# Five more pairs of idle products between the first turns and scores of a tuned attention and FFN kernel

## The chip, the cores and the metric

One core of one Trainium2 chip. The metric is device time in microseconds (us) of one execution, and a profile is one profiled execution with its own trace; times inside it count from the start of its span. TensorE is PE in the profile, VectorE DVE, ScalarE ACT, GpSimd POOL, SyncE SP. "Granted clock" is the share of TensorE's full clock that the trace records as granted.

## The reference

Chunked linear attention with decay, then a highway FFN on its output (cut):

```python
# attention: q, k, v of (4, 8, 768, 64), decay lam per head, blocks of 64
intra = einsum(qb, kb) * Dmask ;  intra = einsum(intra, vb)
inter = einsum(qb * lam_pow, kv_state)
out[block] = intra + inter
kv_state = lam_block * kv_state + einsum(kb * rev_pow, vb)
# FFN on x of (3072, 512)
H = maximum(x @ w_h, 0);  T = sigmoid(x @ w_t + b_t)
return T * H + (1 - T) * x
```

## The kernel before

The kernel builds a list of tasks and issues them in a fixed global order, `ORDER`; each engine gets its own tasks in that order. There are 12 steps, each 256 rows of one batch. A step loads k, q, v, casts or scales them (`kb`, `qb`, `vs`), turns k and q on TensorE, copies the turned tiles out of PSUM, where this kernel's products land (`kT`, `qT`), makes scores, masks them on DVE (`m`), and does intra, state (`kv`) and inter products. FFN products (`block`) and the final turns follow. Steps 0 and 1 are loaded in halves.

The parts that the change and the argument touch:

```python
NF = 12
...
def fill(eng):                                   # an idle pair: its result is never read
    for i in range(2):
        T.matmul(get("fill")[:, i], lhsT=id128, rhs=id128[:, None, :].to_broadcast([128, NP, 128]), start=True, stop=True)

buf(("fill",), "o", [128, 2, NP, C], F32, pool=ps)
for i in range(NF):
    task("fill", fill, writes=[("fill",)])
...
def trans(x, n, p, hs): ...                      # turns: 4 or 8 products of 128x128
def scores(n, u): ...                            # 16 products of 64x64 with 128 columns
def inter(n): ...                                # o <- ss, qT
def block(x, w, g, js): ...                      # FFN: w is wh or wt, the cast weights
...
issued = set()
for i in ORDER:
    t = tasks[i]
    assert all(d in issued for d in t.deps)
    issued.add(t)
    t.emit(t.eng)
```

In the kernel before, all twelve idle pairs come ahead of the first turn, to have TensorE at full clock by then: in its trace the clock is full from 4.21 us, and the first turn starts at 7.97.

## Time and profile before

| | before |
|---|---|
| time, median | 113.19 us (113.16 to 113.62) |
| span of the profiled run, mean granted clock | 110.9 us, 0.950 |
| first turn of step 0, first turn of step 2 | 7.97, 20.64 us |
| clock at half | 14.45 to 24.69 us |
| first FFN product | 24.80 us |

From the first FFN product on TensorE has no gaps to speak of (busy 15.20 of 15.20 us from 24.80 to 40, 20.00 of 20 to 60, 30.00 of 30 to 90), so the moment at which it starts, and the speed of the products before and after it, set the time. The prediction below shows the lines and how they are read.

### The profile page before, as it was taken

The page shows a single profiled execution, that of the slowest core. Times are in us where ns is not written, and L with a number is a line of the kernel's source. Part 1 is how long each engine was busy: PE and PEld are TensorE (multiplying, and loading weights), DVE is VectorE, ACT ScalarE, POOL GpSimd, SP SyncE. Part 2 cuts the span into 40 slices and gives each one's busy share as a digit, 9 for nine tenths or more (in the row PEclk, how much of TensorE's full clock was granted, in tenths as well). Part 3 has the DMA queues.
Part 4 walks back from the last instruction along what each step waited for, and adds up shares of the span by engine and source line. Part 5 has one row for each costly group of instructions (what it writes and reads, how often), then busy time and mean ns, then how long its engine had stood idle before and what let it go on. Part 6 is the DMA issues. An engine that isn't in the chain of part 4 may idle for free.

```text
span 110.9 us, 4776 instructions
## 1 busy us (share of the span) xinstructions
PE 101.5 (92%) x2073; PEld 86.3 (78%) x2073; DVE 78.4 (71%) x128; ACT 72.9 (66%) x137; POOL 63.5 (57%) x55
## 2 busy tenths in 40 slices
PE   4996489689999999999999999999999999999960
PEld 1353469578889889888888889999899888889950
DVE  0179896684998899797778854788775797764630
ACT  3574443177288967668695788787878844785780
POOL 6004626263469899988979979899940040401420
PEclk9999965559999999999999999999999999999998
DMA  0999999999999999999999999999995250024263
GB/s 10 267 292 290 290 293 287 293 356 320 253 290 297 288 292 292 290 294 289 293 287 287 279 292 295 292 264 370 392 343 204 107 188 0 6 101 183 101 236 142
DMA packets 43964, 27.57 MB, mean 249 GB/s; under 512 B 1828, under 2 KB 41000, under 8 KB 43944
## 3 DMA queue, kind: packets, MB, share of 16 engines
q1 hardware_dynamic: 43792, 27.27, 88.3%
q8 instruction: 16, 0.26, 1.0%
q14 instruction: 4, 0.03, 0.1%
q10 hardware_dynamic: 152, 0.01, 0.1%
HBM read 20.98 MB, written 6.29 MB: 246 GB/s over the span
## 4 chain that ended last, share of the span: by engine, by line
PE 76%; SPq 11%; DMA 6%; DVE 2%; issue 1%; POOLq 1%; ACT 0%; DVEq 0%
PE w L293 39%; SPq L208 11%; PE w L315 10%; PE w L223 10%; DMA kf<-in_k_dram 6%; PE w L239 5%; PE o L264 5%; PE kv L272 4%; PE o L252 4%; DVE qT L175 1%; POOLq L469 1%; DVE kb L175 1%; DVE hmx L297 0%; ACT o_sb L173 0%; DVEq L175 0%
## 5 line engine op out<-in xcount | busy, mean ns | idle before, releaser
L293 PE MATMUL w<-xT,w_b 128*128 128x256 bf16 (+1 forms) x416 | 46.9, 265 | 0.0
L293 PEld LDWEIGHTS <-w_b 128*128 128x128 bf16 x416 | 36.5, 98 | 4.4
L243 DVE TENSOR_TENSOR m<-w,tri 128x512 bf16<-128x512 f32 x48 | 30.8, 684 | 4.2 <-PE w L239 3.8
L309 POOL TENSOR_TENSOR th<-t_sb,hmx 128x512 bf16<-128x512 bf16 (+1 forms) x13 | 15.1, 1165 | 23.5 <-DVE hmx L297 14.4
L217 POOL TENSOR_TENSOR vs<-vf,pow_k 128x1024 bf16<-128x1024 f32 (+1 forms) x11 | 20.1, 1824 | 12.2 <-DMA vf<-in_v_dram 11.1
L297 DVE SCALAR_TENSOR_TENSOR hmx<-w,xT 128x512 bf16<-128x512 f32 (+1 forms) x26 | 16.5, 646 | 7.7 <-PE w L293 7.4
L217 POOL TENSOR_TENSOR qb<-qf,pow_q 128x1024 bf16<-128x1024 f32 (+1 forms) x11 | 19.2, 1746 | 4.2 <-DMA qf<-in_q_dram 4.2
L306 ACT ACTIVATE w<-w,bt_col 128x256 f32<-128x256 f32 (+1 forms) x26 | 11.2, 432 | 7.6 <-PE w L293 5.7
L173 ACT ACTIVATE xT<-o 128x512 bf16<-128x512 f32 x22 | 12.1, 597 | 3.7 <-PE o L264 2.3
L173 ACT ACTIVATE kT<-w 128x1024 bf16<-128x1024 bf16 (+1 forms) x11 | 10.0, 906 | 6.9 <-PE w L223 6.9
L315 PE MATMUL w<-id,th 128*128 128x128 bf16 x96 | 12.9, 219 | 0.6 <-POOL th L309 0.6
L239 PE MATMUL w<-qT,kT 64*64 64x128 bf16 x384 | 12.8, 231 | 0.7 <-ACT kT L173 0.3
L315 PE MATMUL w<-id,xT 128*128 128x128 bf16 x96 | 12.9, 220 | 0.0
L173 ACT ACTIVATE o_sb<-w 128x512 f32<-128x512 f32 (+1 forms) x17 | 9.6, 575 | 4.8 <-PE w L315 4.6
L306 ACT ACTIVATE t_sb<-w,bt_col 128x256 bf16<-128x256 f32 (+1 forms) x26 | 10.5, 458 | 3.0 <-PE w L293 3.0
L309 DVE TENSOR_TENSOR th<-w,hmx 128x512 bf16<-128x512 f32 (+1 forms) x13 | 8.4, 648 | 4.2 <-ACT w L306 4.0
L223 PE MATMUL w<-id,kb 128*128 128x128 bf16 x96 | 8.5, 231 | 2.8 <-DVE kb L175 1.4
L272 PE MATMUL kv<-vs,kb 64*64 64x64 bf16 x320 | 10.4, 203 | 0.1
L315 PEld LDWEIGHTS <-th 128*128 128x128 bf16 x96 | 9.4, 98 | 0.9 <-POOL th L309 0.8
L239 PEld LDWEIGHTS <-kT 64*64 64x64 bf16 x384 | 9.1, 112 | 1.2 <-ACT kT L173 0.5
L272 PEld LDWEIGHTS <-kb 64*64 64x64 bf16 x320 | 8.8, 117 | 1.3 <-issue 1.0
L315 PEld LDWEIGHTS <-xT 128*128 128x128 bf16 x96 | 9.3, 98 | 0.5
(46 smaller groups left out, 118.9 us busy)
## 6 DMA issues: line engine op xcount, KB each, us to landing
vf<-in_v_dram SPq DMA_DIRECT2D x24, 256.0 KB, 5.4
kf<-in_k_dram SPq DMA_DIRECT2D x24, 256.0 KB, 5.5
qf<-in_q_dram SPq DMA_DIRECT2D x24, 256.0 KB, 5.5
out_dram<-o_sb SPq DMA_DIRECT2D x23, 256.0 KB, 3.5
w_f<-in_moe_w_t_dram SPq DMA_DIRECT2D x4, 256.0 KB, 6.1
w_f<-in_moe_w_h_dram SPq DMA_DIRECT2D x4, 256.0 KB, 6.2
out_dram<-o_sb SPq DMA_DIRECT2D x2, 128.0 KB, 1.9
lam_bc<-in_lam_dram ACTq DMA_DIRECT2D x1, 4.0 KB, 3.5
```

The lines of the kernel that those rows point to most:

```text
L173: A.activation(dst, src, AF.Copy)
L208: nc.sync.dma_start(out=get(x, n, p)[:, h - hs.start:h - hs.start + 4, :], in_=src[b, h:h + 4, c * 2 * C:(c + 1) * 2 * C, :].rearrange("h ...
L217: ENG[eng].tensor_tensor(dst[:, hs], in0=get(x, n, p).rearrange("p h (j d) -> p h j d", j=J), in1=pw[:, :, :, None].to_broadcast([128, hs. ...
L223: T.transpose(get(x + "tr", n, p)[:, i, j, :], get(x + "b", n)[:, j, h:h + 2, :], id128)
L239: T.matmul(get("s", n, u, e)[half(b), i, j, :], lhsT=turned("k", n)[half(e), hp, b * C + j:(b + 1) * C:J], rhs=turned("q", n)[half(e), hp, ...
L243: V.tensor_tensor(get("m", n, u)[:, e], in0=get("s", n, u, e), in1=tri[:, None].to_broadcast([128, 2, J, C]), op=ALU.mult)
L272: T.matmul(get("kv", n // NST)[half(e), hp, :], lhsT=get("kb", n)[half(b), j, 2 * hp + e, :], rhs=get("vs", n)[half(b), 2 * hp + e, j, :], ...
L293: T.matmul(get(x, g, js[0])[:, i, :], lhsT=w[:, kc, j * 128:(j + 1) * 128], rhs=get("xT", g)[:, kc, :], start=(kc == 0), stop=(kc == KC - 1))
L297: V.scalar_tensor_tensor(get("hmx", g, js[0]), in0=get("h", g, js[0]), scalar=0.0, in1=get("xT", g)[:, js[0]:js[-1] + 1, :], op0=ALU.max, ...
L306: A.activation(get(*gate(g, js))[:, i, :], get("t", g, js[0])[:, i, :], AF.Sigmoid, bias=bt_col[:, j:j + 1])
L309: ENG[TH[js[0] // len(js) % 2]].tensor_tensor(get("th", g)[:, js[0]:js[-1] + 1, :], in0=get(*gate(g, js)), in1=get("hmx", g, js[0]), op=AL ...
L315: T.matmul(get("x", n, b, p)[:, (j - js[0]) * 128:(j - js[0] + 1) * 128], lhsT=get(x, g)[:, j, r * C:(r + 1) * C], rhs=id128, start=(j == ...
```

## The change

The intent is to keep TensorE's clock up. Between the first turns and the first FFN products TensorE has gaps, and the clock falls to half in that stretch. Five more idle pairs are put into the gaps of step 0. The schedule was made anew for it.

```diff
-NF = 12
+NF = 17
 ORDER = [ ... ]      # 537 -> 542 numbers; in TensorE's order this is:
  turn k, part 0
+ fill
  turn q, part 0
+ fill
  turn q, part 1
+ fill
  turn k, part 1
+ fill
  scores, first half
+ fill
  scores, second half
```

Everything else of TensorE's order and of the loads' order is the same. On the other engines some neighbours swap, and two stores change places. Early swaps: DVE scales both halves of step 1's v before it copies xT of step 0 (before: after it). ACT copies a second state (`ss`) of step 0 before its half of xT, and one mask of step 1 comes later on DVE.

## The prediction

> **What bounds the kernel now.** I read four views. First the page, for the strip of 40 slices and the chain that ended last.
>
> ```profile
> PE   4996489689999999999999999999999999999960
> PEclk9999965559999999999999999999999999999998
> DMA  0999999999999999999999999999995250024263
> ...
> PE 76%; SPq 11%; DMA 6%; DVE 2%; issue 1%; POOLq 1%; ACT 0%; DVEq 0%
> ```
>
> One slice is 110.9 / 40 = 2.77 us. From about 25 us to about 105 us TensorE never stops (nines) at full clock, so in that stretch its own work sets the time. Before 25 us it has gaps, and in slices 5 to 8 the granted clock is half. The DMA engines are full from 3 us on. That early stretch is the only place where the change can act.
>
> Second, the chain in order of time, to see what sets the moment at which TensorE becomes continuous:
>
> ```profile
> 12.35 0.83 SPq L208
> 13.18 0.04 issue
> 13.23 6.57 DMA kf<-in_k_dram
> ...
> 19.89 0.70 DVE kb L175
> 20.59 0.05 issue
> 20.64 1.90 PE w L223 x16
> 22.54 0.02 issue
> 22.56 1.24 DVE qT L175
> 23.80 0.04 issue
> 23.84 0.63 PE w L239 x13
> ```
>
> Up to 19.8 us the chain is loads issued one behind the other (0.83 us each), ending with the k block of step 2. Only then come the turns of step 2 (20.64), their copy, the scores (23.84), and at 24.87 the FFN products. What TensorE does before 20.64 is beside the chain as long as it is finished by 20.64.
>
> Third, stretches cut where the clock changes. I looked at 0.1 us steps and found the falls and rises at about 4.2, 14.46 and 24.70 us; the last two are 10.24 us apart, three times 3.41, so I cut in 3.41 us steps through those points. Columns: start:end, length, busy us (and count) of PE, PEld, DVE, ACT, POOL, then granted clock, DMA share, GB/s.
>
> ```profile
> 7.63:11.05 3.42, 2.46 (x51) 1.51 (x49) 3.02 (x7) 1.33 (x3) 1.21 (x2) 1.00 1.22 291
> 11.05:14.46 3.41, 1.64 (x61) 1.36 (x57) 3.12 (x7) 1.45 (x3) 2.43 (x3) 1.00 1.22 290
> 14.46:17.88 3.42, 3.19 (x67) 2.69 (x69) 3.19 (x7) 0.99 (x4) 0.83 (x1) 0.50 1.21 295
> 17.88:21.29 3.41, 2.51 (x55) 2.27 (x55) 1.89 (x4) 0.91 (x2) 1.07 (x1) 0.50 1.04 286
> 21.29:24.70 3.41, 3.09 (x76) 2.75 (x74) 2.50 (x4) 2.34 (x4) 2.10 (x2) 0.50 1.03 341
> ```
>
> A window with PE busy 2.46 of 3.42 us (72%) kept the clock; one with 1.64 (48%) lost it; at half clock 3.19 and 2.51 did not bring it back, and 3.09 did. So busy time alone is not the measure (3.19 failed, 3.09 succeeded): the failing window is mostly 64x64 products, the succeeding one has more 128x128 turns and dense 64x128 ones.
>
> Fourth, PE in order of time around the change:
>
> ```profile
> 7.97 0.39 PE L223 MATMUL w<-id,kb 128*128 128x128 bf16 x4
> 8.20 0.87 PE L223 MATMUL w<-id,qb 128*128 128x128 bf16 x8
> 9.60 0.40 PE L223 MATMUL w<-id,kb 128*128 128x128 bf16 x4 [0.54 <-DVE kb L175]
> 9.93 0.42 PE L239 MATMUL w<-qT,kT 64*64 64x128 bf16 x16
> 10.69 0.42 PE L239 MATMUL w<-qT,kT 64*64 64x128 bf16 x16 [0.34 <-ACT kT L173]
> 12.50 0.40 PE L223 MATMUL w<-id,kb 128*128 128x128 bf16 x4 [1.39 <-POOL kb L175]
> ```
>
> The gaps (0.54, 0.34, 1.39 us) are what the new products are meant to fill.
>
> [...]
>
> **The change, part by part.** It removes nothing. The built programs show TensorE's order unchanged except five added pairs of 128x512 products on the identity: after the turn of k part 0, after q part 0, after q part 1, after k part 1, and between the two halves of the scores, all of step 0. The loads keep their order. Some neighbours swap on the other engines; the one that matters is early on DVE: before, qT, bt_col, xT, then the two vs scalings of step 1; after, qT, vs, vs, xT, bt_col.
>
> Cost of a pair: the last 18 of today's 24 products start between 4.0 and 7.8 us, 3.8 / 17 = 0.22 us each, so 0.44 us a pair, 2.2 us for five. Step by step, with 0.23 us for four turns (7.97 to 8.20) and about 0.3 for 16 scores: k0 7.97 to 8.20, pair to 8.64, q0 to 8.87, pair to 9.31, q1 to 9.54, pair to 9.98, k1 to 10.21 (today starts 9.60), pair to 10.65, first scores start 10.65 (today 9.93), to 10.95, pair to 11.4, second scores 11.4 (today 10.69). So 1.5 us of the 2.2 go into gaps and 0.7 us is pushed down.
>
> The masks start 0.45 us after the scores (10.38 against 9.93): now 11.1; four take 2.48, to 13.6 (was 12.86). qT of step 1 to 14.2. Then the two vs scalings come first; today these run 14.50 to 15.84 on late v data, so they end at 15.5 to 15.8; then xT (0.6) to about 16.4. The first inter products wait for that xT (today's wait: 0.55 us on DVE xT, start 14.63). So they start at about 16.4 instead of 14.63. The run from them to the last scores of step 1 took 5.1 us (14.63 to 19.74), all at half clock.
>
> The window 11.05 to 14.46 gains 0.35 us of added products and the second scores; idle are about 0.7 (11.8 to 12.5) and 0.3 us (13.3 to 13.6), so about 2.4 of 3.41 busy, 70%, near the 72% that kept the clock. I choose "kept" at 60%. The next, to 17.88, then has TensorE idle for nearly 2 us until 16.4 and loses the clock at 17.88. Until then 1.4 us at full clock do 2.8 of those 5.1 us; the rest takes 2.3 us to about 20.2, before 20.64. No loss, no gain yet. The window 17.88 to 21.29 is then denser than today's (less was done before), and may restore the clock at 21.29 instead of 24.70.
>
> What that would be worth: ten of the sixteen turns, the scores (0.63) and the kv products (0.39) at double speed, so the FFN products start at about 23.8 instead of 24.87, 1.1 us earlier. But the third group of the next 32 (27.51 to 31.11, 8 in 0.87 us) starts at 27.51 + 2 x 0.87 = 29.25 and needs the first half of w_t, whose last cast on POOL ran 28.26 to 28.88 behind loads on full DMA engines. So TensorE would stop there for the weights: of 1.1 us at most 29.25 - 28.88 = 0.37 us is left. From there to the end it is work without gaps. The sum: between 0 and -0.4 us.
>
> **The rivals.** (a) The window to 14.46 still falls below the limit (48% lost it, 70% is untested): then the late xT costs, since 16.4 + 5.1 = 21.5 against 20.64: +0.7 to +0.9 us, perhaps recovered by an earlier rise. (b) The clock returns a window later than today (28.1): 3.4 us of FFN products at half speed, 1.7 us more, together +2 us. Against it: that window would be dense work, as the one that succeeded today. (c) The clock never falls: PE's work becomes faster, but the k block still lands at 19.8 and the weights at 28.3, so again -0.4 us. For it: that is the intent; against: nearly 2 us idle before 16.4. (d) The phase of the window differs from run to run: today's timed runs lie within 113.16 to 113.62 and the profiled one took 112.8, so phase is worth under 1 us. (e) The swaps later on cost or give some tenths, since TensorE has no slack there.
>
> **Range and chances.** Weights: about 45% for -0.2 to -0.4, 25% for about 0, 25% for +0.3 to +0.9, 5% for +2. Centre a little below today: 113.1 us, range 112.5 to 114.0. Over 2% faster would need -2.3 us, which the weights' landing forbids: 0.02. Over 2% slower needs rival (b): 0.04. Within 2%: 0.94.
>
> **What would show each step.** Right: scores of step 0 near 10.65 and 11.4; inter products near 16.4 after a wait on DVE xT; clock full across 14.46; k of step 2 still landing near 19.8; FFN products earlier than 24.87 and a new TensorE wait on POOL w_b near 28.9. Wrong: weights that land well before 28, or FFN products that start earlier and whose lead survives to the end (gain above 0.4), or a clock still half after 24.7.

Three things in the text were assumptions when it was written. The step of 3.41 us was one gap of 10.24 us divided by three; the later profiles bear it out, with half-clock stretches of 6.83, 10.24 and 13.65 us (e5, before, e7), two, three and four such steps. That the phase differs from run to run, in rival (d), showed afterwards: the first rise came at 4.21, 5.07 and 5.62 us in three profiles of before. That a window 70% busy would keep the clock, and that there is a "limit", was my estimate from one window that kept it at 72% and one that lost it at 48%; the later windows are not sorted by that share ("Still open" below).

## The result, and the profile after

| | before | changed |
|---|---|---|
| time, median | 113.19 us (113.16 to 113.62) | 111.84 us (111.70 to 112.25) |
| span of the profiled run, mean clock | 110.9 us, 0.950 | 110.2 us, 1.000 |
| first FFN product | 24.80 us | 23.91 us |

The ratio is 0.9878, interval 0.9841 to 0.9914. A ratio is the mean time of one kernel's fast runs over that of the other's of the same rounds, so not quite the ratio of the medians. The change made the kernel faster by 1.2%; I had predicted 113.1 us with a range from 112.5. The measured median lies below the range.

The page of the changed kernel, with the same rows as shown of before: forty slices (PE busy, granted clock, DMA busy), and the chain that ended last by engine.

```profile
PE   4999877579999999999999999999999999999960
PEclk9999999999999999999999999999999999999999
DMA  0999999999999999999999999999997340024264
...
PE 71%; SPq 12%; DMA 6%; POOL 5%; issue 1%; DVE 1%; POOLq 1%; ACT 0%
```

The clock row is where the two pages differ: the 6555 of slices 5 to 8 (counted from 0) is gone. In this profile the clock never falls while there is work.

TensorE in order of time (start, us, engine, line, operation; in brackets the idle time before and who ended it):

```profile
8.30 0.39 PE L223 MATMUL w<-id,kb 128*128 128x128 bf16 x4
8.52 0.59 PE L198 MATMUL o<-id 128*128 128x512 bf16 x2
8.95 0.39 PE L223 MATMUL w<-id,qb 128*128 128x128 bf16 x4
...
11.01 0.42 PE L239 MATMUL w<-qT,kT 64*64 64x128 bf16 x16
11.36 0.60 PE L198 MATMUL o<-id 128*128 128x512 bf16 x2
11.89 0.42 PE L239 MATMUL w<-qT,kT 64*64 64x128 bf16 x16
12.48 0.40 PE L223 MATMUL w<-id,kb 128*128 128x128 bf16 x4 [0.17 <-POOL kb L175]
...
15.33 0.24 PE L252 MATMUL o<-qT,ss 64*64 64x128 bf16 x2 [0.48 <-ACT ss L173]
...
20.62 0.62 PE L223 MATMUL w<-id,kb 128*128 128x128 bf16 x8 [1.48 <-DVE kb L175]
...
23.91 1.92 PE L293 MATMUL w<-xT,w_b 128*128 128x256 bf16 x16
```

The pairs sit where they were meant to, and the wait before the first turn of step 1 has shrunk from 1.39 to 0.17 us. The first inter products (15.33) wait for ACT's ss, not for DVE's xT. The turns of step 2 start at 20.62, as in before (20.64), because the k block lands when it landed before. What follows runs at full speed, so the FFN products come 0.89 us earlier. What ends last ahead of them is no longer the k block. The chain now comes from step 2's v block, which POOL scales before the kv products:

```profile
14.91 6.54 DMA vf<-in_v_dram
21.49 0.09 issue
21.59 1.92 POOL vs L217
23.50 0.04 issue
23.54 0.44 PE kv L272 x16
```

The v block landed at 14.91 + 6.54 = 21.45 us and its scaling ended at 23.51. In this profile a faster TensorE ahead of it could have brought little more: its scores before the kv products ended at 23.00 + 0.42 = 23.42.

The three windows in which the fall could have come, cut at this run's own steps (columns as in the prediction):

```profile
11.69:15.10 3.41, 2.46 (x75) 1.79 (x73) 3.41 (x6) 1.32 (x3) 1.78 (x3) 1.00 1.22 291
15.10:18.52 3.42, 2.58 (x88) 2.12 (x90) 3.42 (x8) 2.14 (x5) 1.49 (x1) 1.00 1.20 292
18.52:21.93 3.41, 1.94 (x54) 1.58 (x56) 2.21 (x5) 0.59 (x1) 0.76 (x2) 1.00 1.02 278
```

They are 72, 76 and 57% busy. The steps do not lie where they lay in before: in that run the clock first rose at 4.21 us, in this one at 4.86, and every later change sits whole steps of 3.41 us after the first rise (in before 14.45 and 24.69 us are three and six steps after it).

POOL's casts of the half of w_t that is loaded last and needed second. It holds the first half of the columns: the prediction calls it "the first half of w_t", the experiments below, by the order of loading, "the second half":

```profile
26.64 0.61 POOL L175 CAST w_b<-w_f 128x512 bf16<-128x512 f32 x1 [0.88 <-DMA w_f<-in_moe_w_t_dram]
27.41 0.62 POOL L175 CAST w_b<-w_f 128x512 bf16<-128x512 f32 x1 [0.16 <-DMA w_f<-in_moe_w_t_dram]
```

They end at 28.03 us, against 28.88 in before. The prediction had let them cap the gain; here the weights came 0.85 us earlier, and the lead of 0.89 us passed them whole.

Later some of the lead is lost. The chain in order of time, at the one place where it leaves TensorE in the middle of the run:

```profile
63.14 1.90 POOL qb L217
65.04 1.46 POOL kb L175
...
66.54 1.07 PE w L223 x16
```

In before these turns start at 67.26, so the lead is 0.72 us here, and 0.65 us at the last wait for DVE's hmx (106.07 against 105.42). That agrees with the spans' difference of 0.7 us. The medians differ by 1.35 us: one profile of each kernel does not hold the whole difference of the timed runs, and the experiments show why.

### The profile page after: what moved, and what is told of

The parts are those of the page before. It is cut to its first block, busy times and chain, and to the rows that moved or that the text cites. A ratio compares the mean times of both kernels' runs of the same rounds, so it can differ in the third digit from the quotient of the medians.

```text
span 110.2 us, 4797 instructions
## 1 busy us (share of the span) xinstructions
PE 100.9 (91%) x2083; PEld 84.4 (77%) x2083; DVE 78.5 (71%) x128; ACT 73.2 (66%) x137; POOL 63.9 (58%) x55
## 4 chain that ended last, share of the span: by engine, by line
PE 71%; SPq 12%; DMA 6%; POOL 5%; issue 1%; DVE 1%; POOLq 1%; ACT 0%
PE w L293 37%; SPq L208 12%; PE w L315 9%; PE w L223 8%; DMA vf<-in_v_dram 6%; PE o L264 5%; PE w L239 4%; PE kv L272 4%; PE o L252 3%; POOL vs L217 2%; POOL qb L217 2%; POOL kb L175 1%; DVE hmx L297 1%; POOLq L469 1%; ACT o_sb L173 0%
## 5 line engine op out<-in xcount | busy, mean ns | idle before, releaser
L239 PE MATMUL w<-qT,kT 64*64 64x128 bf16 x384 | 11.7, 220 | 0.6 <-DVE qT L175 0.6
L198 PE MATMUL o<-id 128*128 128x512 bf16 x34 | 10.0, 439 | 1.4 <-POOL id masks.py:199 1.4
L272 PE MATMUL kv<-vs,kb 64*64 64x64 bf16 x320 | 9.4, 194 | 0.4 <-DVE ss L175 0.3
L239 PEld LDWEIGHTS <-kT 64*64 64x64 bf16 x384 | 8.3, 106 | 1.6 <-issue 1.3
L223 PE MATMUL w<-id,kb 128*128 128x128 bf16 x96 | 7.7, 220 | 1.9 <-DVE kb L175 1.5
```

Source lines behind the costliest of these rows:

```text
L223: T.transpose(get(x + "tr", n, p)[:, i, j, :], get(x + "b", n)[:, j, h:h + 2, :], id128)
L239: T.matmul(get("s", n, u, e)[half(b), i, j, :], lhsT=turned("k", n)[half(e), hp, b * C + j:(b + 1) * C:J], rhs=turned("q", n)[half(e), hp, ...
L272: T.matmul(get("kv", n // NST)[half(e), hp, :], lhsT=get("kb", n)[half(b), j, 2 * hp + e, :], rhs=get("vs", n)[half(b), 2 * hp + e, j, :], ...
```

## The experiments

My theory after the result: the pairs keep the clock, the swaps do nothing for it, and how much that gives depends on how early the weights land. The rivals: the swap that frees the inter products gives the gain (swaps); it was luck in the phase (phase: how long after the start of the span the first rise comes, 4.16 to 7.22 us in these profiles; a window is a stretch of 3.41 us counted from it); what counts is something other than busy time (work). Order edits are given as TensorE's or the loads' order, since the numbers of `ORDER` tell nothing. Every run was correct. In the lists of clocks, mean clock 1.00 is no half-clock time; 0.969 is about 6.8 us of it, as (1 - 0.969) x 110.5 / 0.5, two windows; 0.954 is about 10.2 us, three windows, part of which can lie after the last product. The mean leaves out the time before the first rise, which the records do not cover.

**e1_fills_only** (the kernel before, with the pairs alone)

```diff
-NF = 12
+NF = 17
+ the five pairs at the changed kernel's places; other engines keep before's order
```

> The kernel before, in its own order, with nothing but the five added pairs at the same five places of TensorE's order (TensorE's order is then that of the changed kernel, the other engines keep theirs). Clock theory: [...]the granted clock stays at or near 1.00 through 25 us, the first FFN product starts near 24.0 us and the time is 0.985 to 0.991 of before, as the changed kernel's 0.988. Swap rival (the gain comes from the first inter products being freed of their wait for DVE's xT): 0.997 to 1.003, because that wait is in this kernel again.

Ratio 0.9946 (0.9879 to 1.0013). Mean clocks 0.954, 0.966, 0.969, 0.969, 1.00, 1.00; the eleven runs of before in these rounds 0.939 to 0.955. The clock half of the expectation holds in part: five of six runs lie above every run of before (the sixth was a slow run), but only two kept the clock throughout. The gain in time is unclear and smaller than expected. The profiled run shows one reason: its first rise was at 4.40 us, the clock fell at 18.05 and came back at 24.88. TensorE around that:

```profile
20.68 1.04 PE L223 MATMUL w<-id,kb 128*128 128x128 bf16 x8 [0.74 <-DVE kb L175]
...
24.88 1.92 PE L293 MATMUL w<-xT,w_b 128*128 128x256 bf16 x16
```

The turns of step 2 are at half clock and the FFN products start where they start in before (24.80). I infer that a half clock that ends before 20.6 us would cost little, and that one that covers 20.6 to 24.9 costs the gain in the FFN products' start; no run isolates either.

**e2_swaps_only** (the changed kernel without the five pairs)

```diff
-NF = 17
+NF = 12
- the five pairs; other engines keep the changed kernel's order
```

> The changed kernel without the five added pairs: only the swaps among neighbours on the other engines are left. Clock theory: the clock falls near 14.5 us as before and stays half for two or three windows (mean clock about 0.95), time 0.997 to 1.004 of before. Swap rival: 0.985 to 0.992.

Ratio 1.0075 (1.0012 to 1.0138). Mean clocks 0.939 to 0.954 in all six runs, as before. Alone the swaps neither keep the clock nor give the gain; they are a little slower, more than I expected. With e1 this settles that the pairs are what changes the clock. Whether the swaps add to the time once the pairs are there is not separated: the interval of e1 overlaps that of the changed kernel.

**e3_fills_in_hole** (the kernel before, three pairs in one gap)

```diff
  scores of step 0, second half
+ fill, fill, fill
  turn k of step 1
```

> The kernel before with three pairs (six products, about 1.3 us) in one place only: after the second scores of step 0, in the 1.39 us gap before the first turn of step 1. No score and no mask is delayed by them. Clock theory by share of busy time: the window that fell with 1.64 of 3.41 us busy has about 2.9 then, the clock stays up there, but the later gaps (14.1 to 14.6, 17 to 20.6) are as in before; the changed kernel held the clock with a window 57% busy, so it should hold here too: mean clock 0.97 to 1.00 and 0.985 to 0.993 of before. A rival, that the clock needs dense work from the first turns on (7.6 to 11 us) and not a filled gap later: falls as before, 0.997 to 1.003.

Ratio 0.9965 (0.9883 to 1.0048) from three fast runs; three others were slow. Clocks 1.00, 0.992, 0.985, 0.97, 0.956, 0.941. Filling one later gap can keep the clock too, in some runs: the three fast ones have 0.985 to 1.00, as expected, but their time misses the range and is not told from before's. The profiled run kept it throughout, with its FFN products at 23.72, and shows the cap of my prediction at work:

```profile
26.36 1.92 PE L293 MATMUL w<-xT,w_b 128*128 128x256 bf16 x16
28.80 1.92 PE L293 MATMUL w<-xT,w_b 128*128 128x256 bf16 x16 [0.52 <-POOL w_b L175]
```

Here the weights were cast at 28.74 us and TensorE, ready earlier, waited 0.52 us for them.

**e4_w_t_late** (the changed kernel, two loads later)

```diff
  loads: w_t first half, w_h
+ q of step 3
  w_t second half
- q of step 3
```

> The changed kernel with the two loads of the second half of w_t moved behind the two q loads of step 3: the weights land about 1.5 us later, nothing else moves. In the changed kernel the cast of the piece needed first ends at 28.03 and its products start about 28.37, so 0.34 us of room. If the landing of these weights is what caps the gain (my prediction's cap), TensorE stops for about 1.2 us there and the time is 1.009 to 1.012 of the changed kernel, that is 0.997 to 1.000 of before. If the room is larger than I think, or the wait is made up later, 0.986 to 0.990 of before.

Ratio 1.0055 (0.9975 to 1.0136) against before, from three fast runs. No run of the changed kernel shared the rounds. In the profile the products stop at the weights:

```profile
27.66 1.92 PE L293 MATMUL w<-xT,w_b 128*128 128x256 bf16 x16
30.62 1.59 PE L293 MATMUL w<-xT,w_b 128*128 128x256 bf16 x13 [1.04 <-POOL w_b L175]
```

The stop that I had put at about 1.2 us measured 1.04; the time is above the expected 0.997 to 1.000, with an interval that reaches into it. The weights are the next limit, with little room behind the FFN products' start. The step of the prediction that used this limit was right in kind.

**e5_after_again** (no edit: the changed kernel, in later rounds)

> The changed kernel as it is, once more, beside before on one chip and beside the three kernels below. In the runs so far the kernel before and the one with the swaps alone had a mean clock of 0.94 to 0.955 in every run, the kernels with the five pairs 0.954 to 1.00, so the clock theory expects at least four of six runs at 0.966 or above (two half windows or none) and 0.982 to 0.993 of before. [...]the clock is at 0.955 in most runs and the time at 0.995 to 1.003 of before.

The clause cut from the last sentence was its condition, the rival that the first result was luck in the phase.

Ratio 0.9959 (0.9912 to 1.0007), an interval that holds 1. Clocks 0.969 five times and 0.981; before 0.954 in ten of eleven runs, and 0.969 in one, which took 111.83 us, less than any run of the changed kernel here. In the first result three of four runs had 1.00. So in all six runs of these rounds the change takes a window or more off the usual half-clock time, but the full clock of the first result was, as I read it, a favourable set of phases. In the profiled run the first rise was at 5.81 us; the clock fell at 16.05 and returned at 22.88, and the FFN products started at 24.57.

**e6_front** (the same products, another place)

```diff
+ fill x5
  turn k of step 0, part 0     # all 17 pairs ahead of it, before's order otherwise
```

> The kernel before with the five pairs all ahead of the first turn (17 pairs of warm-up instead of 12), none between the turns and scores. The same products, another place: every turn and score of step 0 comes 2.2 us later, while the first turn of step 1 still waits for POOL's kb at 12.5 us. Clock theory: the gap at 11 to 12.5 us shrinks likewise because the work moves into it, so the clock may hold (0.96 to 1.00), but masks start about 1.3 us later than in before and xT with them; if that passes into the turns of step 2 the gain is gone: 0.990 to 1.003. Rival (placement between turns is what keeps the clock): mean clock 0.94 to 0.955 and 1.000 to 1.008.

Ratio 1.0276 (1.0202 to 1.0350), a clear loss, and larger than either side expected; clocks 0.926 to 0.964. The first turn starts at 11.27 us, the turns of step 2 at 23.89 instead of 20.64, and the FFN products at 27.70:

```profile
11.27 0.39 PE L223 MATMUL w<-id,kb 128*128 128x128 bf16 x4
...
23.89 1.03 PE L223 MATMUL w<-id,kb 128*128 128x128 bf16 x8 [0.23 <-DVE kb L175]
```

DVE, which copies and masks step 0 late, then casts k of step 2 late. Where the idle products stand matters more than that they are there.

**e7_two_pairs** (the changed kernel without the first three of the five pairs)

```diff
-NF = 17
+NF = 14
```

> The changed kernel with only two of the five pairs, those ahead of the first scores and between the two halves of the scores. About 1.3 us less idle work. If the clock is a matter of the share of a window that is busy, two pairs leave the window around 8 to 12 us near 75% and the one after at about 55 to 60%: mean clock between the two, some runs at 0.95 and some at 0.97 to 1.00; time 0.988 to 0.998 of before. If all five are needed: 0.94 to 0.955 and 0.997 to 1.004.

Ratio 1.0130 (1.0049 to 1.0211). Clocks 0.932 to 0.970, in two groups as expected, but the time misses: slower than before. The one profile is of a slow run: its clock was half from 16.64 to 30.29 us, over the first FFN products (from 26.31). The fast runs at 0.968 to 0.970 took 113.43 to 114.53 us, and no trace of them exists. So the clock alone does not explain the time of this kernel, and this stays open.

**e8_hold_and_early** (the changed kernel with six idle products before the turns of step 2, and step 2's intra products earlier)

```diff
  scores of step 1, second half
+ six products into a score buffer
  turn k of step 2
...
+ intra of step 2
  FFN products that need the second half of w_t
- intra of step 2
```

> The changed kernel with two additions: six idle products (1.3 us) in the gap that TensorE has before the turns of step 2 (19.1 to 20.6 us), in a score buffer, and the intra products of step 2 moved ahead of the first product that needs the second half of w_t. The first is to hold the clock in those phases of the window in which the changed kernel still lost it (0.969): at least five of six runs at 0.99 to 1.00. The second fills the wait for late weights (0.52 us in the run with the filled hole). Against the changed kernel of the same rounds: 0.993 to 0.999. If the turns of step 2 are delayed by the idle products, 1.000 to 1.005.

Ratio 1.0025 (0.9954 to 1.0095); clocks 0.967 three times, 0.97, 0.981, 0.996. The clock had already fallen when the idle products came, so they ran at half speed and pushed the turns from 20.6 to 22.90:

```profile
20.63 2.44 PE L438 MATMUL w<-id 128*128 128x512 bf16 x6
22.90 0.61 PE L223 MATMUL w<-id,kb 128*128 128x128 bf16 x8
```

Six idle products took 2.44 us here, after the clock was lost; in e3, at full clock, six took 1.47 us.

**e9_before_copy_a** and **e10_before_copy_b** (no edit: two more profiles of before)

> The kernel before, unchanged, for a second profile of it: where the first rise of the clock falls (4.21 us in the first profile; 4.4 to 6.7 in the other kernels' profiles) is outside the kernel's control. [...]the first turn starts at 7.97 + (rise - 4.21) / 2, falls and rises of the clock sit whole 3.41 us steps after the rise, and the first FFN product starts later than 24.80 where the rise is later, by up to 1 us. If the phase does not matter, the FFN products start at 24.6 to 25.0 whatever the rise.

> The same once more, for a third phase: same expectation as the run before.

The first rises were at 5.62 and 5.07 us, and the first turns at 8.67 and 8.40, exactly the formula. The half stretches were 12.45 to 22.69 and 11.89 to 22.13 us, whole steps after the rise. The FFN products started at 24.59 and 24.30: earlier than 24.80, so that part misses. My reading, from three profiles, is that a half stretch that ends earlier counts for more than a first turn that starts later. One kernel unchanged gives spans of 110.3, 110.9 and 111.7 us in three profiles; the last had further short gaps in mid-run, so its span is not the phase alone.

**e11_early_a** (the changed kernel with step 2's intra products ahead of the products that need the second half of w_t)

```diff
+ intra of step 2
  FFN products that need the second half of w_t
- intra of step 2
```

> The changed kernel with the intra products of step 2 moved ahead of the first product that needs the second half of w_t, and no idle products added. It costs TensorE nothing and takes away the wait for weights where the FFN products come early and the weights late (0.52 us seen). Where there was no such wait nothing changes. Against the changed kernel: 0.995 to 1.000; against before 0.984 to 0.994. If the masks of step 2 are not ready in time, TensorE waits for DVE there and it is 1.000 to 1.005 of the changed kernel.

Ratio 0.9875 (0.9817 to 0.9934) against before, as expected; clocks 1.00 four times and 0.963 twice. No run of the changed kernel shared these rounds; e15 makes that comparison.

**e12_ten_ahead** (the changed kernel with two warm-up pairs fewer)

```diff
-NF = 17
+NF = 15      # ten pairs ahead of the first turn, the five between as they are
```

> The changed kernel with ten pairs ahead of the first turn instead of twelve. Where the clock rises late the two pairs cost 1.7 us at half clock and push every turn and score of step 0; without them the first turn starts 0.4 us (early rise) to 0.85 us (late rise) earlier. If that lateness is what costs the runs with a late rise, 0.990 to 0.998 of the changed kernel, 0.980 to 0.992 of before. If the pairs ahead are needed for the first rise or the clock falls more often, mean clock 0.94 to 0.96 and 0.997 to 1.010 of before.

The 1.7 us is an estimate from before's trace, where the products of the pairs start (4.0 - 1.42) / 6 = 0.43 us apart ahead of the first rise and 0.22 us apart after it.

Ratio 0.9943 (0.9871 to 1.0015), clocks 0.939 to 0.981. Not the gain expected, and not the loss either: inconclusive.

The last four runs share their rounds.

**e13_quarter** (the five pairs on a quarter of the array)

```diff
-task("fill", fill, writes=[("fill",)])
+task("fill", fill if i < 12 else fillq, writes=[("fill",)])
+# fillq: lhsT=id128[0:64, 0:64], rhs on 64 rows, the same 512 columns
```

> The changed kernel with its five added pairs made on 64 rows and 64 columns of the array instead of 128 and 128: the same 512 columns streamed in the same 0.22 us each, a quarter of the array at work. If TensorE's busy time keeps the clock, nothing changes: mean clock 0.966 to 1.00 in most runs, time as the changed kernel of the same rounds (0.998 to 1.002 of it). If the amount of array work keeps it (the pairs then count 1280 full columns instead of 5120), the clock falls one window earlier as in before: mean clock 0.94 to 0.955 in most runs and 1.004 to 1.012 of the changed kernel.

Ratio 0.9883 (0.9814 to 0.9953) from three fast runs, with clocks 0.992, 0.993, 0.996; the three slow ones had 0.969, 0.969, 0.970. None is below the lowest of the changed kernel beside it (0.954). The fall that the expectation called for, if array work counts, did not come. But its one profile could hardly have shown it: the first rise was late (7.22 us), and the two windows in which the quarter pairs stand (7.22 to 14.04) hold 6400 and 3584 full columns (columns streamed times the share of the array used), more than any window that lost the clock in the count under "Still open" below. Nor was the edit neutral in time: a turn with its pair took 0.86 us (9.46 to 10.32), against 0.65 in the changed kernel (8.30 to 8.95). So the run misses its expectation and decides little between busy time and array work.

**e14_changed_third** (no edit)

> The changed kernel, in the same rounds as the three others, as their measure: mean clock 0.966 to 1.00, 0.985 to 0.996 of before.

Ratio 0.9923 (0.9864 to 0.9981). Clocks 0.954, 0.962, 0.963, 0.969, 0.970, 1.00. The profiled run was a slow one, so its time is compared with nothing; its clock is of use, because its first rise, at 4.16 us, is next to the 4.21 that my prediction was built on. Its windows:

```profile
14.40:17.81 3.41, 2.33 (x93) 1.91 (x86) 3.25 (x7) 1.85 (x4) 0.78 (x2) 1.00 1.21 292
17.81:21.23 3.42, 2.52 (x56) 2.18 (x50) 2.53 (x5) 0.38 (x1) 1.29 (x1) 0.50 1.18 314
21.23:24.64 3.41, 3.09 (x75) 2.69 (x74) 2.50 (x4) 2.52 (x4) 1.90 (x1) 0.50 1.04 338
24.64:28.05 3.41, 3.41 (x17) 2.22 (x16) 1.36 (x3) 1.86 (x5) 1.26 (x3) 0.50 1.04 302
```

Full across 14.4, lost at 17.8, half until 28.05: in this phase the changed kernel does what the prediction said at 17.88, and then its rival (b), though the window that lost the clock was 2.33 of 3.41 us busy and its longest gap was 0.60 us, not nearly 2. Two runs of before in these rounds had clocks of 0.983 and 0.998 and took 113.06 and 113.07 us, no faster than its runs at 0.954. I have no trace of them and can't say what held them up.

**e15_early_a_again** (e11's kernel)

> The kernel with the intra products of step 2 moved forward, again, now beside the changed kernel: 0.995 to 1.000 of it if the wait for the late weights is what it removes (0.5 us in the runs that have it, nothing in the others), 0.984 to 0.994 of before.

Ratio 0.9926 (0.9879 to 0.9973) against before. Against the changed kernel of the same rounds the fast means are 112.38 and 112.34 us, 1.000: it beats before, not the changed kernel.

**e16_hold_by_work** (e11's kernel with two more pairs where TensorE waits)

```diff
-NF = 17
+NF = 18
+ fill, ahead of the intra products of step 0
+ two products into a score buffer, ahead of the last kv products of step 1
```

> The same with one more pair ahead of the intra products of step 0 and one pair (in a score buffer) ahead of the last kv products of step 1, both where TensorE waits about 0.4 us. The windows that still lost the clock in the changed kernel counted 2720 to 2816 full columns, the one after 2304 to 2550; a pair adds 1024. If array work above some 2900 columns keeps the clock, the mean clock is 0.98 to 1.00 in at least five of six runs and the time 0.993 to 0.999 of the changed kernel. If the count is not what matters, it falls as often as the changed kernel's (0.963 to 0.97), and the pairs cost 0 to 0.5 us.

The 2900 columns are my estimate, put just above the counts of 2720 to 2816 in windows that lost the clock.

Ratio 0.9907 (0.9856 to 0.9957). Clocks 0.996, 0.996, 0.997, 0.997, 1.00, and one 0.970. The profiled run had a late first rise, 6.79 us, and kept the clock to the end:

```profile
PEclk9999999999999999999999999999999999999998
```

Five of six runs are within the clock expected, so the two pairs do for the clock what they were meant to. Against the changed kernel the fast means are 112.09 and 112.34 us, 0.998, which these rounds do not tell from 1. So holding the clock in nearly every run is possible, but no version here is shown to beat both kernels.

### What the phases show together

| profile | first rise | half clock | first FFN product | span |
|---|---|---|---|---|
| before | 4.21 | 14.45 to 24.69 | 24.80 | 110.9 |
| before, e10 | 5.07 | 11.89 to 22.13 | 24.30 | 110.3 |
| before, e9 | 5.62 | 12.45 to 22.69 | 24.59 | 111.7 |
| changed | 4.86 | none | 23.91 | 110.2 |
| changed, e5 | 5.81 | 16.05 to 22.88 | 24.57 | 110.6 |
| changed, e14 (slow) | 4.16 | 17.82 to 28.05 | 24.60 | 112.2 |
| pairs alone, e1 | 4.40 | 18.05 to 24.88 | 24.88 | 110.8 |

Over the three comparisons the changed kernel's runs with a mean clock of 1.00 average 111.72 us (four), the fast ones with 0.969 average 112.37 us (seven). Before's fast runs at 0.954 in the last four sets of rounds average 112.96 us (eighteen). These cross chips, so they are an order, not a law.

The phase acts in a second way, which the table does not show. In the profiles of e5 (first rise 5.81), e15 (6.10) and e13 (7.22) the chain that ended last no longer holds a load of step 2. It runs from the warm-up through the turns and masks of step 0: DVE's cast of step 2's k starts at 20.02, 20.59 and 21.16 us, against 19.87 in the changed kernel's first profile. With so late a rise TensorE and DVE are themselves late, so, as I read it, the added pairs no longer hide behind the loads.

## Why the prediction was wrong, point by point

**Wrong: "The next, to 17.88, then has TensorE idle for nearly 2 us until 16.4 and loses the clock at 17.88."** Two things failed in it. First, "The first inter products wait for that xT" was carried over from before. In the changed order the inter products stand ahead of the xT copy, and TensorE's first inter product carries no wait for DVE; it waited 0.48 us for ACT's ss and began at 15.33, although xT itself was as late as predicted (15.78 to 16.47). So the idle stretch of nearly 2 us did not exist, and the gap there was 0.48 us. Second, the place of the window was read from one profile and taken for the changed kernel's. In the one changed run that had nearly that phase (e14, 4.16 us) the clock fell at 17.82: there the moment came out right without the reason given for it. In the profiled result (4.86) it did not fall; in e5 (5.81) it fell at 16.05.

**Wrong in size: rival (d), "phase is worth under 1 us".** I read it off four runs of before. It ought to have widened the range. Before loses the clock in almost every phase (41 of its 44 later runs have a mean of 0.955 or less), so its times hide what phases do; the changed kernel goes from no half-clock time to three windows of it. Its three comparisons gave 0.9878, 0.9959 and 0.9923, on average 0.992. The first had three of four runs at full clock, all sixteen runs of that kernel only four. Part of the miss is thus that the sample was favourable, and the later medians, 112.23 and 112.76 us, lie on either side of my lower end.

**Wrong as a number: "at most 29.25 - 28.88 = 0.37 us is left".** The limit exists: e3 waited 0.52 us at it and e4, with the weights moved back, 1.04 us. But I took the landing as fixed. In the result the cast ended at 28.03; in the kernel before itself the last of these casts started at 28.26, 27.7 and 27.4 us in its three profiles. What moves it is argued, not isolated: one 16 KB instruction load falls into the same stretch. The DMA queues of 20 to 22 us, for before and then for the changed kernel (packets, MB, share of 16 engines' time):

```profile
q8 instruction: 1, 0.02, 5.4%
```

```profile
q8 instruction: 1, 0.02, 3.5%
```

That packet took 0.054 x 2 x 16 = 1.73 us in one and 1.12 us in the other. But its length does not sort the landings: in e1's profile it took 0.034 x 2 x 16 = 1.09 us (20 to 22 us), and the last of these casts still ended at 27.07 + 1.38 = 28.45, later than in the changed kernel. No experiment moved it alone, and the cause stays open.

**Right.** A pair costs 0.44 us (8.52 to 8.95 here). With the first turn at 8.30 instead of 7.97 (the late rise), the steps predicted for the first scores, the masks and the vs scalings come out within 0.1 us: 10.65 + 0.33 against 11.01, 11.1 + 0.33 against 11.46, and the vs scalings end at 15.84. The window in which before lost the clock kept it, as I chose (11.69 to 15.10 here, 10.99 to 14.40 in e14). In this profile the k block of step 2 set the turns at 20.62 whatever TensorE did before, so most of the recovered clock bought nothing; with a late first rise this does not hold (above). The FFN products were predicted at 23.8 if the clock were up again by then, and came at 23.91. The prediction looked at the right stretch, the half clock of 14.45 to 24.69 us, and gave the outcome "kept throughout" no weight of its own beyond rival (c), which it capped at 0.4 us.

**The range and the chances.** The chances of the three classes were right (within 2%). The range was too narrow above all on the fast side, since I held both the window's phase and the weights' landing to the values of one trace.

**Still open.** What decides whether the clock falls is not shown. Share of busy time does not sort the windows: in these profiles, windows that lost the clock were 46 to 69% busy, and windows that kept it went down to 56%. A count of columns streamed times the share of the array used sorts most of them. Taken over all eighteen profiles, with each product counted in the window in which it starts, the fourteen windows that lost the clock hold 1536 to 2816 full columns, and those that kept it 2816 or more. Counted by its end instead, the groups overlap (lost up to 3584, kept from 2688), so this is an order in these traces and not a rule that is shown; e16 agrees with it, e13 does not decide. Open too are the times of e7 and of before's two runs at 0.983 and 0.998.

## What to carry to other kernels

Here idle products paid where they filled waits that TensorE had anyway, by 0.4 to 1.2% in three comparisons of which one does not exclude zero; the same products ahead of that work cost 2.8%. As I read the profiles, what they can gain depends on how much of the half-clock stretch covers work on the critical chain (half until 24.88 us and FFN products at 24.88 in e1, no half clock and 23.91 in the changed kernel). Where the first rise moves from profile to profile, here from 4.16 to 7.22 us, it has to be read from several, and a prediction should be worked out for more than one phase. When a schedule is made anew, look up each wait in the new order instead of carrying it over.
